# Seven block products in place of eight, and one step for the remainder, in the cosine layer of a Fourier and two-layer network kernel

## The chip, the core and the metric

The kernel runs on one core of one Trainium2 chip. Its engines work side by side: TensorE (PE in the rows; PEld is its weight load), VectorE (DVE), ScalarE (ACT), GpSimd (POOL) and SyncE (SP), which here only starts transfers. They share SBUF, and TensorE writes its sums to PSUM, in which the kernel takes tiles of one or two banks of 128 x 512 floats, and VectorE and ScalarE read them there. The metric is the device time of the whole launch in microseconds; less is better.

## The reference

`x` is 4 x 3008 tokens of 256 values, `w_in` is 256 x 2048 and `w_out` is 2048 x 256 in both layers, all of it in 32-bit floats:

```
X = Re FFT(FFT(x, axis=1), axis=2)             # attn, per batch
t = relu(X @ moe_w_in)                         # layer 1
x2 = (t * t) @ moe_w_out
h = x2 @ moe2_w_in                             # layer 2, first product
y = (h * cos(h)) @ moe2_w_out                  # layer 2, second product
```

## The kernel before, in words

Every product keeps float precision by splitting each factor into a high and a low part in the 32-bit matmul format: wh x xh, wh x xl and wl x xh, three matmuls on TensorE for one product. Tokens lie along the columns, features along the 128 partitions. The real part of the transform pairs a token with its mirror image, so the work goes by pairs: `BLOCKS` holds 12 blocks of 512, 512 and 480 pairs (the last 484), and the first product of layer 1 gives a sum and a difference from which `l1_add` makes both tokens of a pair.

Layer 1 runs over 12 blocks x 16 slices of 128 hidden features: `l1_mm1` (6 matmuls, line 550), `l1_add` (three VectorE operations, lines 557 and 235, the latter in the helper `tt`), `l1_act` (three ScalarE operations, lines 567 to 570), `l1_lo` (four GpSimd pieces, line 580) and `l1_mm2` (12 matmuls, line 592). At a block's end `l1_out` (lines 608 to 621) makes a high and a low part of the sums and stores both to the array `o_dram`, of which `load_o` reads both parts for layer 2.

Layer 2 runs over `HALVES`, 24 groups of up to 512 columns, x `NS` = 8 steps of two slices each. A step is `l2_mm1` (12 matmuls, lines 635 to 645) into a PSUM tile of two banks (one of the two `h` buffers, or every third time `acc1`), `l2_n` (ScalarE, line 650: h / 2 pi rounded to an integer n), `l2_r` (VectorE, line 658, twice: r = h - n C1 - n C2, with C1 + C2 = 2 pi), `l2_cos` (ScalarE, lines 665 and 666: the absolute value and the sine that gives the cosine), `l2_g` (VectorE, lines 671 and 235: times h), `l2_hi` (ScalarE, line 676) and `l2_lo` (GpSimd, line 683): the high and low part of the result g, and `l2_mm2` (12 matmuls, line 695) into `acc0`; after eight steps `l2_out` (lines 698 to 705) copies the sums out and stores them.

The weights of layer 2 are converted from their 64-bit form during layer 1 by `conv_w2`, stored, and loaded back by `load_w2` when layer 2 nears. No scheduler decides the order: every piece of work is registered by `at(t, fn, name)` with a time in units of steps, the table `TIMES` replaces some of these times by name, and `od.issue()` sorts all of them and writes the instructions. Each engine then runs its own in that order. A step's second product stands 4.3 steps behind its first one (`LAG + 1.3`, with 3 for `LAG`), and the other stages lie between.

Of the kernel before, what the change touches and what calls it, by code (L numbers as in the profile page):

```python
# [91 lines left out]

@with_exitstack
def kernel(ctx: ExitStack, tc: tile.TileContext, x, x128, cs, tab0, tab1, w_in1, w_out1, w_in2, w_out2, out):
    nc = tc.nc
# [539 lines left out]
    def l2_mm1(k, i):
        w = HALVES[k][1]
        hi, lo = xt[2, k]
        step = NS * k + i
        a = ps_a.tile([P, 2, BLK], F32, name="acc1") if step > LAG and step % 3 == 1 else ps_h.tile([P, 2, BLK], F32, name="h")
        for j in range(2):  # L640
            for m in range(2):
                wh, wl = (w_in_t([c[p] for c in wi2], m, 2 * i + j) for p in range(2))
                for q, (st, mv) in enumerate(((wh, hi), (wh, lo), (wl, hi))):
                    nc.tensor.matmul(a[:, j, :w], st, mv[:, m, :w], start=m == 0 and q == 0, stop=m == 1 and q == 2)  # L644
        hs[k, i] = a
# [365 lines left out]
```

## Time and profile before

| | us |
|---|---|
| three runs | 1927.09, 1930.08, 1930.56 |
| their median | 1930.08 |
| span of the profiled execution | 1925.3 |
| TensorE busy | 1886.7 (98%) |
| ScalarE busy | 1481.3 (77%) |
| VectorE busy | 1341.9 (70%) |
| GpSimd busy | 1074.6 (56%) |

The span runs from the first to the last instruction that the profiler recorded; the time of a run has in addition what lies around it. Layer 1 gives way to layer 2 between about 883 and 896 us of the span: before that stand the transform and layer 1, behind it some 1,025 us of layer 2. Durations in the rows are of single instructions or of short runs of them (x4 stands for four in a row).

### The profile page before, as it was taken

How to read it: one execution, taken by the hardware profiler on the slowest of the kernel's cores; microseconds unless marked ns; L12 is line 12 of the kernel's file. 1: busy time of each engine (PE TensorE's matmuls, PEld its weight loads, DVE VectorE, ACT ScalarE, POOL GpSimd, SP SyncE). 2: the span in 40 equal slices, each digit the busy share in tenths (PEclk: the TensorE clock that was granted, in tenths of full speed). 3: DMA queues.
4: the chain of work that ended last, by engine and by line, in shares of the span. 5: the costliest groups of instructions: out<-in, count | busy, mean ns of one | idle time of the engine just before them, and what ended most of it. 6: DMA issues, size and time to landing. Idle time of an engine off the chain costs nothing.

```text
span 1925.3 us, 23825 instructions
## 1 busy us (share of the span) xinstructions
PE 1886.7 (98%) x8544; PEld 1571.1 (82%) x8544; DVE 1341.9 (70%) x1566; ACT 1481.3 (77%) x1537; POOL 1074.6 (56%) x1004
## 2 busy tenths in 40 slices
PE   5899999999999999999999999999999999999999
PEld 3678888888888888888888888888888888888887
DVE  6889858768576776666666666666666666666666
ACT  3788778777788888887777777777777777777776
POOL 1667778777677777774444444444444444444442
PEclk9899999999999999999999999999999999999999
DMA  8564434334434434344011011100110001011100
GB/s 278 177 245 148 157 111 165 141 123 168 149 131 128 150 107 140 116 162 159 33 43 44 33 32 33 44 32 32 46 42 33 32 32 43 33 34 34 52 12 21
DMA packets 76345, 177.85 MB, mean 92 GB/s; under 512 B 9168, under 2 KB 32736, under 8 KB 76132
## 3 DMA queue, kind: packets, MB, share of 16 engines
q1 hardware_dynamic: 73812, 168.27, 25.9%
q0 software_dynamic: 1840, 6.73, 1.1%
q8 instruction: 67, 1.10, 0.2%
q10 hardware_dynamic: 576, 1.35, 0.2%
q14 instruction: 50, 0.41, 0.1%
HBM read 117.53 MB, written 63.42 MB: 94 GB/s over the span
## 4 chain that ended last, share of the span: by engine, by line
PE 81%; DVE 1%; issue 0%; ACT 0%; DVEq 0%; ACTq 0%
PE acc L695 27%; PE h L644 18%; PE acc L592 18%; PE acc L644 9%; PE h L550 9%; PE h L333 1%; DVE s L235 0%; DVE inT L235 0%; DVE u L557 0%; DVE ol L235 0%; ACT oh L618 0%; DVE o L703 0%; ACT o L702 0%; DVEq L235 0%; DVE dl L235 0%
## 5 line engine op out<-in xcount | busy, mean ns | idle before, releaser
L683 POOL TENSOR_TENSOR gl<-r,gh 128x1024 fp32r<-128x1024 f32 (+2 forms) x189 | 445.4, 2356 | 574.5 <-ACT gh L676 564.5
L580 POOL TENSOR_TENSOR gl<-s,gh 128x256 fp32r<-128x256 f32 (+2 forms) x768 | 591.2, 801 | 218.9 <-ACT gh L570 194.0
L658 DVE SCALAR_TENSOR_TENSOR r<-n,h 128x1024 f32<-128x1024 int32 (+2 forms) x129 | 154.7, 1199 | 219.1 <-ACT n L650 201.3
L567 ACT ACTIVATE s<-s 128x1024 f32<-128x1024 f32 (+2 forms) x192 | 199.5, 1039 | 89.3 <-DVE s L235 88.8
L235 DVE TENSOR_TENSOR s<-u,h 128x512 f32<-128x512 f32 (+2 forms) x384 | 242.8, 674 | 25.7 <-POOL gl L580 3.8
L650 ACT ACTIVATE n<-h 128x1024 int32<-128x1024 f32 (+2 forms) x129 | 130.3, 1010 | 160.5 <-PE h L644 160.4
L592 PE MATMUL acc<-gh,wbh 128*128 128x512 f32 (+2 forms) x768 | 237.2, 390 | 0.7 <-DVE ol L235 0.7
L592 PE MATMUL acc<-gl,wbh 128*128 128x512 f32 (+2 forms) x768 | 235.9, 388 | 1.4 <-POOL gl L580 1.3
L658 DVE SCALAR_TENSOR_TENSOR r<-n,r 128x1024 f32<-128x1024 int32 (+2 forms) x192 | 231.6, 1206 | 6.6
L592 PE MATMUL acc<-gh,wbl 128*128 128x512 f32 (+2 forms) x768 | 235.1, 387 | 0.0
L557 DVE SCALAR_TENSOR_TENSOR u<-zb,wc,h 128x512 f32<-128x512 f32 (+2 forms) x192 | 140.6, 732 | 130.2 <-PE h L550 129.2
L666 ACT ACTIVATE r<-r,halfpi 128x1024 f32<-128x1024 f32 (+2 forms) x192 | 218.3, 1137 | 6.2
L568 ACT ACTIVATE s<-s 128x1024 f32<-128x1024 f32 (+2 forms) x192 | 200.6, 1045 | 6.1
L570 ACT ACTIVATE gh<-s 128x1024 fp32r<-128x1024 f32 (+2 forms) x192 | 200.5, 1044 | 6.1
L695 PE MATMUL acc<-gh,wbh 128*128 128x512 f32 (+2 forms) x768 | 202.9, 386 | 0.0
L695 PE MATMUL acc<-gh,wbl 128*128 128x512 f32 (+2 forms) x768 | 202.9, 386 | 0.0
L695 PE MATMUL acc<-gl,wbh 128*128 128x512 f32 (+2 forms) x768 | 202.8, 386 | 0.0
L644 PE MATMUL h<-xh,wah 128*128 128x512 f32 (+2 forms) x516 | 199.2, 386 | 0.0
L644 PE MATMUL h<-xl,wah 128*128 128x512 f32 (+2 forms) x516 | 199.2, 386 | 0.0
L644 PE MATMUL h<-xh,wal 128*128 128x512 f32 (+2 forms) x516 | 199.1, 386 | 0.0
L665 ACT ACTIVATE r<-r 128x1024 f32<-128x1024 f32 (+2 forms) x192 | 198.2, 1032 | 0.0
L676 ACT ACTIVATE gh<-r 128x1024 fp32r<-128x1024 f32 (+2 forms) x192 | 197.1, 1027 | 1.1 <-DVE r L658 0.8
(125 smaller groups left out, 3257.6 us busy)
## 6 DMA issues: line engine op xcount, KB each, us to landing
inT<-x_in SPq DMA_DIRECT2D x18, 512.0 KB, 7.6
oh<-oh SPq DMA_DIRECT2D x16, 512.0 KB, 3.5
ol<-ol SPq DMA_DIRECT2D x16, 512.0 KB, 2.8
xh<-oh SPq DMA_DIRECT2D x16, 512.0 KB
xl<-ol SPq DMA_DIRECT2D x16, 512.0 KB, 4.7
y_out<-o SPq DMA_DIRECT2D x32, 256.0 KB, 2.1
mid<-w_in SPq DMA_DIRECT2D x14, 511.5 KB, 4.4
mid<-w_out SPq DMA_DIRECT2D x14, 511.0 KB, 4.1
```

The costliest lines, as they stand in the source:

```text
L235: nc.vector.tensor_tensor(out=out, in0=in0, in1=in1, op=op)
L567: nc.scalar.activation(s[:, :, :w], s[:, :, :w], AF.Relu)
L568: nc.scalar.activation(s[:, :, :w], s[:, :, :w], AF.Square)
L570: nc.scalar.activation(hi[:, :, :w], s[:, :, :w], AF.Copy)
L580: nc.gpsimd.tensor_tensor(out=lo[:, n, cols], in0=s[:, n, cols], in1=f32(hi)[:, n, cols], op=ALU.subtract)
L592: nc.tensor.matmul(accs[1, k][m][:, n, :w], wt, g[:, n, :w], start=begin and i == 0, stop=end and i == 2)
L644: nc.tensor.matmul(a[:, j, :w], st, mv[:, m, :w], start=m == 0 and q == 0, stop=m == 1 and q == 2)
L658: nc.vector.scalar_tensor_tensor(out=r[:, :, :w], in0=n[:, :, :w], scalar=-c, in1=src[:, :, :w], op0=ALU.mult, op1=ALU.add)
L665: nc.scalar.activation(r[:, :, :w], r[:, :, :w], AF.Abs)
L666: nc.scalar.activation(r[:, :, :w], r[:, :, :w], AF.Sin, bias=halfpi, scale=-1.0)
L683: e.tensor_tensor(out=lo[:, :, :w], in0=r[:, :, :w], in1=f32(hi)[:, :, :w], op=ALU.subtract)
L695: nc.tensor.matmul(accs[2, k][:, m, :w], w_out_t([c[part] for c in wo2], f, m), g[:, j, :w], start=f == 0 and q == 0, stop=f == NF - 1 and ...
```

## The change

**Seven products.** The weights' slices of a step (two, each 256 deep) and a span of columns form a 2 x 2 grid of blocks on either side: A is w_in of layer 2 (rows are the two slices, columns the two halves of the depth), B is x2 (rows are the halves of the depth, columns two groups of tokens). In place of the eight products A_ik B_kj the new code takes seven, M1 to M7, of sums of blocks. `SPANS` has 12 spans of 512 column pairs (the last 388) in place of the 24 groups, so that a span's two groups are the two column blocks. Sums on the weights' side (S1 to S4) are made once in layer 1, by `sums_w2`. Sums on the side of x (T1X to T4X) are made for every span by `diff`, on GpSimd (on VectorE for the first), and each of the seven right-hand factors is then split by `x_hi` (ScalarE, line 700) and `x_lo` (VectorE, line 704).

**Two banks with partial sums.** The products go to two single banks, b0 and b1. In b0 stand M1, then M1 + M6, then that + M7, then that + M4, which is the corner C21 of the result; in b1 M5, then M5 + M3, and then anew M2. Between them partial sums are copied to SBUF: x1 = M1 (ScalarE, line 730), x2 = M1 + M6 and x5 = M5 (VectorE, line 732). The corners of h are then C12 = b1 + x2, C11 = b1 + x1 and C22 = b0 + x5 (VectorE, `tt`, line 237) and C21 = b0 (ScalarE, line 742), all in SBUF.

**The remainder in one step.** `l1_out` now scales by 1 / 2 pi (a ScalarE pass, line 668, and a VectorE pass, line 669, for the two parts of the constant) and stores one float array. So h comes in turns, and n is h rounded, in a pair of PSUM banks `pp` (line 747), the remainder r = h - n is one operation (line 751), and the sine takes 2 pi as its scale (line 757), without an absolute value. `l2_g` of the first slice pair stays on VectorE and that of the second goes to GpSimd (line 762); high part line 768, low part line 773. n1, r1, c1, g1, h1, l1 and n2 to l2 name these stages for the two row blocks. `l2_mm2` comes in eight pieces m0 to m7 of three matmuls (line 785), so that they can stand between the products. `l2_out` multiplies by 2 pi.

**The order.** A step now has 16 x 128 x 128 blocks of work on two groups of columns, as two steps had before. Its length is `STEP` = 2.5 of the units of `at`, and a table `OFF` places each piece. `l1_mm1` takes its three matmuls in another order, its last two slices go to `pp`, and layer 1's last five second products stand among the first products of layer 2, which begin 1.5 units before layer 1's last slot. From `TIMES` eight entries of the steps 187 to 192 are gone.

The core of the diff:

```diff
-HALVES = [(2 * c + n * w, w) for c, w in BLOCKS for n in range(2)]
+SPANS = [(c, min(BLK, NPAIR - c)) for c in range(0, NPAIR, BLK)]
-    o_dram = [dram.tile([2, P, NCOL], F32, name=f"o{p}") for p in "hl"]
+    o_dram = dram.tile([2, P, 2, NPAIR], F32, name="o")
...
+    def sums_w2(c, j):
...
+            tt(o[0], b[1][0], b[1][1], ALU.add)
+            tt(o[1], o[0], b[0][0], ALU.subtract)
+            tt(o[2], b[0][0], b[1][0], ALU.subtract)
+            tt(o[3], b[0][1], o[1], ALU.subtract)
...
     def l1_out(k, m):
-        nc.scalar.activation(hi, src, AF.Copy)
-        tt(lo, src, f32(hi), ALU.subtract)
...
+        nc.scalar.activation(o, src, AF.Copy, scale=PER2)
+        nc.vector.scalar_tensor_tensor(out=o, in0=src, scalar=PER1, in1=o, op0=ALU.mult, op1=ALU.add)
+        nc.sync.dma_start(out=o_dram[m][:, :, c:c + w], in_=o)
...
+    def diff(k, j, e):
+        a, b = {T1X: ("b12", B11), T3X: (B22, "b12"), T2X: (B22, T1X), T4X: (B21, T2X)}[j]
+        e.tensor_tensor(out=cols_of(k, j), in0=cols_of(k, a), in1=cols_of(k, b), op=ALU.subtract)
+    def x_hi(k, j):
...
+        nc.scalar.activation(x[:, 0], cols_of(k, j), AF.Copy)
+    def x_lo(k, j):
+        x = right[k, j]
+        nc.vector.tensor_tensor(out=x[:, 1], in0=cols_of(k, j), in1=f32(x)[:, 0], op=ALU.subtract)
+    M1, M2, M3, M4, M5, M6, M7 = (A11, B11), (A12, B21), (S4, B22), (A22, T4X), (S1, T1X), (S2, T2X), (S3, T3X)
+    def product(k, i, b, pair_of, start):
...
+        for q, (st, mv) in enumerate(((wl, 0), (wh, 1), (wh, 0))):
+            nc.tensor.matmul(bank["b"][b][:, :w], st, x[:, mv], start=start and q == 0, stop=q == 2, skip_group_check=True)
+    def copy_of(k, i, x, b, e):
...
+        src = bank["b"][b][:, :w]
+        if e is nc.scalar:
+            nc.scalar.activation(u, src, AF.Copy)
+        else:
+            nc.vector.tensor_copy(u, src)
+    def corner(k, i, j, n, b, x):
+        src, dst = bank["b"][b][:, :SPANS[k][1]], h_of(k, i, j)[:, n]
+        if x is None:
+            nc.scalar.activation(dst, src, AF.Copy)
+        else:
+            tt(dst, src, us[k, i, x], ALU.add)
     def l2_n(k, i, j):
-        nc.scalar.activation(n[:, :, :w], hs[k, i][:, :, :w], AF.Copy, scale=1.0 / (2.0 * math.pi))
+        nc.scalar.activation(bank["p"].bitcast(I32)[:, :, :SPANS[k][1]], hs[k, i, j], AF.Copy, bias=0.25)
     def l2_r(k, i, j):
-        for c, src in ((C1, hs[k, i]), (C2, r)):
-            nc.vector.scalar_tensor_tensor(out=r[:, :, :w], in0=n[:, :, :w], scalar=-c, in1=src[:, :, :w],
-                                           op0=ALU.mult, op1=ALU.add)
+        nc.vector.scalar_tensor_tensor(out=r, in0=bank["p"].bitcast(I32)[:, :, :SPANS[k][1]], scalar=-1.0, in1=hs[k, i, j],
+                                       op0=ALU.mult, op1=ALU.add)
     def l2_cos(k, i, j):
-        nc.scalar.activation(r[:, :, :w], r[:, :, :w], AF.Abs)
-        nc.scalar.activation(r[:, :, :w], r[:, :, :w], AF.Sin, bias=halfpi, scale=-1.0)
+        dst = r if j else bank["p"][:, :, :SPANS[k][1]]
+        nc.scalar.activation(dst, r, AF.Sin, bias=halfpi, scale=TURN)
     def l2_g(k, i, j):
-        tt(r[:, :, :w], r[:, :, :w], h[:, :, :w], ALU.mult)
+        if j:
+            (V if ends(k, i) else G).tensor_tensor(out=r, in0=r, in1=h, op=ALU.mult)
+        else:
+            tt(r, bank["p"][:, :, :SPANS[k][1]], h, ALU.mult)
...
+    OFF = {"M5": -0.267, "x5": -0.173, "M1": 0.0, "M3": 0.133, "x1": 0.154, "M6": 0.267, "x2": 0.362, "C12": 0.447, "M7": 0.467,
+           "M2": 0.533, "C11": 0.635, "C22": 0.701, "n1": 0.757, "M4": 0.8, "r1": 0.893, "C21": 0.895, "n2": 1.052, "r2": 1.177,
+           "c1": 1.321, "c2": 1.431, "g1": 1.513, "g2": 1.567, "h1": 1.656, "l1": 1.818, "m0": 1.867, "h2": 1.951, "l2": 2.075,
+           "m1": 2.2, "m2": 2.334, "m3": 2.401, "m4": 2.601, "m5": 2.668, "m6": 2.934, "m7": 3.068}
...
+            hi = {B11: 2.82, B22: 3.82, T1X: 4.82, T2X: 6.82, T3X: 7.3, B21: 7.82, T4X: 8.3}
+            lo = {B11: 3.76, B22: 4.76, T1X: 5.76, T2X: 7.32, T3X: 7.76, B21: 8.32, T4X: 8.34}
+            dif = {T1X: 4.5, T3X: 5.5, T2X: 6.5, T4X: 7.5}
```

How the order stands, on TensorE in the middle of layer 2. Before, twelve matmuls of the first product (line 644) stand in one block, ahead of and behind twelve of the second (line 695); the rows are the end of one block of each:

```order
L644 MATMUL acc1_8897<-xh_8603,wah_7941 128x512
L644 MATMUL acc1_8897<-xl_8604,wah_7941 128x512
L644 MATMUL acc1_8897<-xh_8603,wal_7942 128x512
L695 MATMUL acc0_8650<-gh_8855,wbh_8326 128x512 [waits Activation_49]
L695 MATMUL acc0_8650<-gh_8855,wbh_8326 128x512 x3
L695 MATMUL acc0_8650<-gh_8855,wbl_8327 128x512 x4
L695 MATMUL acc0_8650<-gl_8857,wbh_8326 128x512 [waits Pool_49]
L695 MATMUL acc0_8650<-gl_8857,wbh_8326 128x512 x3
L644 MATMUL h_8944<-xh_8603,wah_8074 128x512 [waits DVE_49,PE_49]
```

After, at a boundary of two spans: the products M5, M4 and M1 (line 713, by the banks that they write) stand with units of three or six of the second product (line 785) around them:

```order
L713 MATMUL b1_8151<-x_8593,wal_7814 128x512 [waits DVE_49]
L713 MATMUL b1_8151<-x_8593,wah_7813 128x512 x2
L713 MATMUL b0_8150<-x_8867,wal_7814 128x512 [waits DVE_49,Activation_49]
L713 MATMUL b0_8150<-x_8867,wah_7813 128x512 x2
L785 MATMUL acc0_8359<-gh_8895,wbh_8385 128x512 [waits Activation_49]
L785 MATMUL acc0_8359<-gh_8895,wbh_8385 128x512
L785 MATMUL acc0_8359<-gh_8895,wbl_8386 128x512
L785 MATMUL acc1_8415<-gh_8843,wbh_8385 128x512 x2
L785 MATMUL acc1_8415<-gh_8843,wbl_8386 128x512
L713 MATMUL b0_8150<-x_8436,wal_7814 128x512 [waits Activation_49]
L713 MATMUL b0_8150<-x_8436,wah_7813 128x512 x2
```

What moved: the first product no longer stands in blocks of twelve into banks of its own; every third or sixth matmul belongs to another bank, and most groups of the first product wait for a reader of the bank that they write.

VectorE, at the same place. Before, a step holds two remainders and one product with h:

```order
L658 SCALAR_TENSOR_TENSOR r_10200<-n_10198,acc1_10172 128x1024 [waits Activation_49,Pool_49]
L658 SCALAR_TENSOR_TENSOR r_10200<-n_10198,r_10200 128x1024 [waits DVE_49]
L235 TENSOR_TENSOR r_10156<-r_10156,h_10125 128x1024 [waits Activation_49]
L658 SCALAR_TENSOR_TENSOR r_10237<-n_10235,h_10210 128x1024 [waits Activation_49,Pool_49]
L658 SCALAR_TENSOR_TENSOR r_10237<-n_10235,r_10237 128x1024 [waits DVE_49]
L235 TENSOR_TENSOR r_10200<-r_10200,acc1_10172 128x1024 [waits Activation_49]
```

After, from x2 to x5 and the two remainders, with the splits of x (line 704) of the next span between them:

```order
L732 COPY x_8792<-b0_8150 128x512 [waits PE_49]
L237 TENSOR_TENSOR h_8798<-b1_8151,x_8792 128x512 [waits DVE_49]
L237 TENSOR_TENSOR r_8755<-pp_8152,h_8717 128x1024 [waits Activation_49]
L237 TENSOR_TENSOR h_8798<-b1_8151,x_8775 128x512 [waits PE_49]
L237 TENSOR_TENSOR h_8818<-b0_8150,x5_8750 128x512
L704 TENSOR_TENSOR x_8785<-oin_8374,x_8785 128x512
L732 COPY x5_8832<-b1_8151 128x512 [waits DVE_49,PE_49]
L751 SCALAR_TENSOR_TENSOR r_8837<-pp_8152,h_8798 128x1024 [waits Activation_49,Pool_49]
L751 SCALAR_TENSOR_TENSOR r_8859<-pp_8152,h_8818 128x1024 [waits Activation_49,Pool_49]
L704 TENSOR_TENSOR x_8830<-oin_8375,x_8830 128x512
L704 TENSOR_TENSOR x_8867<-oin_8374,x_8867 128x512 [waits Activation_49]
```

What moved: the copies and corners stand on VectorE between the stages of the cosine, and a split stands ahead of x5, or behind the second remainder and so ahead of the next x2.

TensorE where the layers meet. Before, the first product of layer 1's last slices (line 550) alternates with blocks of its second product (line 592), and the first product of layer 2 follows in blocks of twelve; after, M5, M4 and M1 of layer 2 stand directly behind each other, between blocks of twelve of layer 1's second product (now line 644):

```order
L713 MATMUL b1_8151<-x_7946,wal_7814 128x512 [waits DVE_49]
L713 MATMUL b1_8151<-x_7946,wah_7813 128x512 x2
L713 MATMUL b0_8150<-x_8102,wal_7814 128x512 [waits DVE_49]
L713 MATMUL b0_8150<-x_8102,wah_7813 128x512 x2
L713 MATMUL b0_8150<-x_7870,wal_7814 128x512 [waits Activation_49]
L713 MATMUL b0_8150<-x_7870,wah_7813 128x512 x2
L644 MATMUL acc0_7765<-gh_8191,wbh_1315 128x484 x2
L644 MATMUL acc0_7765<-gh_8191,wbl_1316 128x484 x2
L644 MATMUL acc0_7765<-gl_8193,wbh_1315 128x484 [waits Pool_49] x2
```

What moved: M1 of a step follows M4 of the step before without another matmul between them.

## Rows read from the trace of the kernel before

**Rows 1.** The page's first part: busy us of each engine, share of the span, instructions.
```profile
PE 1886.7 (98%) x8544; PEld 1571.1 (82%) x8544; DVE 1341.9 (70%) x1566; ACT 1481.3 (77%) x1537; POOL 1074.6 (56%) x1004
```

**Rows 2.** Stretches, us: PE, PEld, DVE, ACT, POOL busy (instructions), PEclk, DMA share, GB/s.
```profile
750.00:800.00 50.00, 50.00 (x221) 41.31 (x220) 33.62 (x52) 43.22 (x45) 38.07 (x51) 1.00 0.39 131
1000.00:1050.00 50.00, 50.00 (x223) 41.43 (x222) 33.92 (x30) 38.19 (x39) 21.60 (x9) 1.00 0.09 31
```

**Rows 3.** Timeline of PE in layer 2 (start us, duration us), line 695.
```profile
942.51 1.07 PE L695 MATMUL acc<-gh,wbh 128*128 128x512 f32 x4
...
947.95 1.07 PE L695 MATMUL acc<-gh,wbh 128*128 128x512 f32 x4
...
1083.11 1.03 PE L695 MATMUL acc<-gh,wbh 128*128 128x480 f32 x4
...
1088.31 1.03 PE L695 MATMUL acc<-gh,wbh 128*128 128x480 f32 x4
```

**Rows 4.** Groups by line and shape, 910 to 1910: busy us, mean ns | idle before.
```profile
L683 POOL TENSOR_TENSOR gl<-r,gh 128x1024 fp32r<-128x1024 f32 x126 | 302.3, 2399 | 378.4 <-ACT gh L676 378.4
...
L666 ACT ACTIVATE r<-r,halfpi 128x1024 f32<-128x1024 f32 x124 | 143.1, 1154 | 4.0
L676 ACT ACTIVATE gh<-r 128x1024 fp32r<-128x1024 f32 x126 | 131.5, 1044 | 0.0
...
L235 DVE TENSOR_TENSOR r<-r,h 128x1024 f32<-128x1024 f32 x82 | 99.5, 1214 | 0.0
L658 DVE SCALAR_TENSOR_TENSOR r<-n,h 128x1024 f32<-128x1024 int32 x81 | 98.9, 1221 | 140.4 <-ACT n L650 135.3 <-POOL gl L683 5.1
L650 ACT ACTIVATE n<-h 128x1024 int32<-128x1024 f32 x81 | 83.3, 1029 | 102.6 <-PE h L644 102.5
...
L703 DVE COPY o<-acc 128x512 f32<-128x512 f32 x16 | 11.1, 692 | 1.1
...
L702 ACT ACTIVATE o<-acc 128x512 f32<-128x512 f32 x16 | 9.2, 577 | 0.0
```

**Rows 5.** Waits, 910 to 1910: engine and line, whom for: us, times, longest.
```profile
ACT n L650 <- PE h L644: 157.0, 124, 1.5
```

**Rows 6.** Timeline of one step of layer 2, with the wait in brackets.
```profile
1007.56 0.39 PE L644 MATMUL h<-xh,wal 128*128 128x512 f32 x1
...
1007.99 1.03 ACT L650 ACTIVATE n<-h 128x1024 int32<-128x1024 f32 x1 [1.33 <-PE h L644]
...
1009.12 1.22 DVE L658 SCALAR_TENSOR_TENSOR r<-n,h 128x1024 f32<-128x1024 int32 x1 [1.83 <-ACT n L650]
```

**Rows 7.** Timelines of two places in layer 1 where engines follow each other.
```profile
880.30 0.72 DVE L557 SCALAR_TENSOR_TENSOR u<-zb,wc,h 128x484 f32<-128x484 f32 x1 [1.02 <-PE h L550]
881.15 1.23 DVE L235 TENSOR_TENSOR s<-u,h 128x484 f32<-128x484 f32 x2
...
51.38 1.29 DVE L235 TENSOR_TENSOR s<-u,h 128x512 f32<-128x512 f32 x2 [2.25 <-POOL gl L580]
...
52.72 0.50 PE L550 MATMUL h<-xh,wah 128*128 128x512 f32 x1 [1.90 <-DVE s L235]
...
53.06 0.39 PE L550 MATMUL h<-xl,wah 128*128 128x512 f32 x1
```

**Rows 8.** Tile dl (count: shortest/median/longest ns, first, last start), then a timeline.
```profile
L235 DVE TENSOR_TENSOR dl<-inT,dh x18: 685/1053/1287, 180.8 to 469.2; 128x512 fp32r<-128x512 f32 x18
L235 DVE TENSOR_TENSOR dl<-in,dh x4: 687/690/692, 26.1 to 41.2; 128x512 fp32r<-128x512 f32 x4
...
886.36 2.72 POOL L580 TENSOR_TENSOR gl<-s,gh 128x242 fp32r<-128x242 f32 x4 [0.27 <-ACT gh L570]
...
888.48 1.68 DVE L658 SCALAR_TENSOR_TENSOR r<-n,r 128x1024 f32<-128x1024 int32 x1
```

**Rows 9.** Groups by line and shape, 0 to 900, of layer 1.
```profile
L580 POOL TENSOR_TENSOR gl<-s,gh 128x256 fp32r<-128x256 f32 x512 | 400.2, 814 | 151.2 <-ACT gh L570 136.8 <-DVE s L235 6.0 <-PE acc L333 5.3
...
L235 DVE TENSOR_TENSOR s<-u,h 128x512 f32<-128x512 f32 x256 | 164.6, 685 | 18.7 <-POOL gl L580 3.8 <-DVE u L557 0.9 <-POOL zl L405 0.2
```

More of the change, by code (lines that the diff above doesn't have):

```diff
@@ L520, in load_w2, with left @@
         (wi2 if name == "in" else wo2).append(parts)
+    win, wie = {}, []
+    A11, A12, A22, S1, S2, S3, S4 = range(7)
+    def left(j, i):
+        c, s = i // 2, i % 2
+        if j < S2:
+            return [p[:, j * 2 * P + s * P:j * 2 * P + (s + 1) * P] for p in wi2[c]]
+        return [p[:, j - S2, s * P:(s + 1) * P] for p in wie[c]]
     gs, accs = {}, {}
-    xt, uv, ss = {}, {}, {}
+    xt, uv, ss, bank = {}, {}, {}, {}
     parts, part_dram = {}, {}
@@ L635, in l2_mm1 @@
[L635 to L645, printed above, removed]
@@ L679, in l2_lo @@
-    def l2_lo(k, i, e=nc.gpsimd):
-        w = HALVES[k][1]
-        hi, r = gs[2, k, i], rs.pop((k, i))
-        lo = buf("gl2", "gl", F32R, late["pool"], 4)
-        e.tensor_tensor(out=lo[:, :, :w], in0=r[:, :, :w], in1=f32(hi)[:, :, :w], op=ALU.subtract)
-        gs[2, k, i] = hi, lo
-    def l2_mm2(k, i):
-        w = HALVES[k][1]
-        if i == 0:
-            accs[2, k] = ps_a.tile([P, 2, BLK], F32, name="acc0")
-        hi, lo = gs.pop((2, k, i))
-        for q, (part, g) in enumerate(((0, hi), (1, hi), (0, lo))):
-            for m in range(2):
-                for j in range(2):
-                    f = 2 * i + j
-                    nc.tensor.matmul(accs[2, k][:, m, :w], w_out_t([c[part] for c in wo2], f, m), g[:, j, :w],
-                                     start=f == 0 and q == 0, stop=f == NF - 1 and q == 2)
@@ new lines, in x_hi @@
+    def x_hi(k, j):
+        tag = XTAGS[(7 * k + j) % 10]
+        x = buf(tag, "x", F32R, late["pool"] if tag in ("cv", "xc") else work, XTAGS.count(tag))[:, :, :SPANS[k][1]]
+        right[k, j] = x
+        nc.scalar.activation(x[:, 0], cols_of(k, j), AF.Copy)
[3 more added lines that the diff above has]
+    M1, M2, M3, M4, M5, M6, M7 = (A11, B11), (A12, B21), (S4, B22), (A22, T4X), (S1, T1X), (S2, T2X), (S3, T3X)
@@ new lines, in l2_hi, with l2_lo, l2_mm2 @@
+    def l2_hi(k, i, j):
+        gs[2, k, i, j] = hi = gh_buf()[:, :, :SPANS[k][1]]
+        nc.scalar.activation(hi, rs[k, i, j], AF.Copy)
+    def l2_lo(k, i, j):
+        hi, r = gs[2, k, i, j], rs.pop((k, i, j))
+        lo = (buf("B1", "gl", F32R) if j and i % 2 else gl_buf())[:, :, :SPANS[k][1]]
+        (V if ends(k, i) else G).tensor_tensor(out=lo, in0=r, in1=f32(hi), op=ALU.subtract)
+        gs[2, k, i, j] = hi, lo
+    def l2_mm2(k, i, n):
+        m, j, half = n // 4, n // 2 % 2, n % 2
+        w = SPANS[k][1]
+        if i == 0 and j == half == 0:
+            accs[2, k, m] = ps_a.tile([P, 2, BLK], F32, name=f"acc{m}")
+        f = 2 * i + j
+        hi, lo = gs[2, k, i, j]
+        for q in range(3 * half, 3 * half + 3):
+            part, g = ((0, hi), (1, hi), (0, lo))[q // 2]
+            nc.tensor.matmul(accs[2, k, m][:, q % 2, :w], w_out_t([c[part] for c in wo2], f, m), g[:, q % 2],
+                             start=f == 0 and q < 2, stop=f == NF - 1 and q >= 4)
@@ L858, with open_banks @@
             else:
-                at(i + LAG - 0.55, lambda k=k, m=m: l1_out(k, m), ("out", k, m))
+                at(i + LAG - 0.55 if k < NB - 1 else L2S + 4.05 + 0.4 * m, lambda k=k, m=m: l1_out(k, m), ("out", k, m))
                 if f0:
                     at(i + LAG - 2, lambda k=k, m=m: load_part(k, m), ("load_part", k, m))
+    def open_banks():
+        h_ctx.close()
+        ps_b = ctx.enter_context(tc.tile_pool(name="ps_b", bufs=1, space=PSUM))
+        bank["b"] = [ps_b.tile([P, BLK], F32, name=f"b{n}") for n in range(2)]
+        bank["p"] = ps_b.tile([P, 2, BLK], F32, name="pp")
     def open_late():
@@ L871 @@
         conv_w2(OPEN + 1.5 + SPAN * i, SPAN, *job)
-    T2S = NF * NB
+    at(T2S - 2.25, open_banks)
     for c in range(NCH):
@@ L981, in _token_columns @@
         pair = b * JB + np.arange(JB)
-        k = np.searchsorted([c for c, _ in BLOCKS], pair, side="right") - 1
-        c, w = (np.array([BLOCKS[i][n] for i in k]) for n in range(2))
-        plus = c + pair
-        minus = plus + w
+        plus = pair
+        minus = NPAIR + pair
         own, mirrored = np.where(flip, plus, minus), np.where(flip, minus, plus)
```

211 lines of the change are left out of this document (143 added, 68 removed).

## The prediction

> **What bounds the kernel now.** I read the busy shares first [rows 1]: TensorE is busy for 98% of the span, so the reader looks there first and asks whether it also runs without gaps. The busy time by stretches says yes: in layer 1 and in layer 2 alike a stretch of 50 us holds 50.00 us of TensorE at a granted clock of 1.00, the upper level, while VectorE has 34 us, ScalarE 38 and GpSimd 22 in layer 2 [rows 2]. The waits of layer 2 agree: its six rows name ScalarE, VectorE and GpSimd as those who wait, one of them ScalarE for the product h [rows 5], and TensorE in none. So the time of layer 2 is the number of matmul slots times the length of a slot. One block of 24 matmuls takes 947.95 - 942.51 = 5.44 us at 512 columns, 0.2267 us a slot, and 5.20 us, 0.2167 a slot, at 480 [rows 3]; the two differ by 0.3125 ns a column, so I take 0.2179 for 484 columns and 0.188 for 388.
>
> **Matmul slots: -64.3 us.** Before, layer 2 has 24 column groups of 8 steps with 24 matmuls: 192 x (16 x 0.2267 + 6 x 0.2167 + 2 x 0.2179) = 1029.7 us. After, it has 12 spans of 8 steps, and the order shows 45 matmuls in a step, 21 for the first product (7 x 3) and 24 for the second: 360 x (11 x 0.2267 + 0.188) = 965.4 us. The difference is 64.3 us, and it is worth its full length only if nothing makes TensorE wait.
>
> **A full step of 10.20 us, and what has to fit.** The seven products go through two banks that are read half-way, so TensorE now depends on a read within its own step. I count in units of three matmuls, 0.68 us. From its order, M1 begins at 0, M3 at 1.36, M6 at 2.72, M7 at 4.76, M2 at 5.44, M5 of the next step at 7.48, M4 at 8.16, M1 again at 10.20; second-product units fill the rest. A reader starts 0.20 us after the last slot ends (1007.79 to 1007.99), VectorE 0.10 after ScalarE ends [rows 6], VectorE 0.13 after its own earlier result, and TensorE 0.05 after VectorE, with a first slot that is 0.11 longer [rows 7]. The operations are priced by the nearest rows: copy from PSUM 0.69 on VectorE and 0.58 on ScalarE [rows 4], a sum with a PSUM input 0.69 [rows 9].
> - M6 to M7 through the copy x2: 0.20 + 0.69 + 0.16 = 1.05 of 1.36 us, 0.31 to spare.
> - M6 to M2 through x2 and the sum C12: 0.20 + 0.69 + 0.13 + 0.69 + 0.16 = 1.87 of 2.04, 0.17 to spare, the tightest.
> - M2 to M5 through C11: 1.05 of 1.36, 0.31 to spare. M4 to M1 through the ScalarE copy C21: 0.94 of 1.36, 0.42 to spare. M1 to M6 through x1: 0.94 of 2.04.
>
> The one shared pair of banks pp passes through two roundings, two remainders, a sine and a product: 2 x 1.03 + 2 x 1.22 + 1.15 + 1.21 [rows 4] and six handoffs of about 0.1, 7.5 us of 10.2. ScalarE has 2 x (1.03 + 1.15 + 1.04) + 2 x 0.58 and about 0.7 for the splits of x and the output, 8.3 us; VectorE 5 x 0.69 + 2 x 1.22 + 1.21 and about 0.9, 8.0; GpSimd 3 x 2.40 and 0.6 for the differences of x, 7.8. Two operations have no row. Rounding into PSUM: the nearest row rounds out of it, 1.03; 1.0 to 1.5 lies within the spare time of that chain. A multiplication on GpSimd: nearest is its subtraction, 2.40; from a little less up to 3.4 it stays hidden, since the second product wants that result about a microsecond after it is there. One remainder step for two and no absolute value remove work only from engines that nobody waited for: 0 us by themselves, but without them VectorE would hold 10.4 us and ScalarE 10.4, more than a step.
>
> So a bare step fits, and its cost is 0.
>
> **The splits of x: +18 us (3 to 38).** Seven times in a span VectorE subtracts with both inputs in SBUF (L704), placed between the operations above. Such a subtraction of 512 columns took 0.69 us in the early stage and 1.05 in the median beside a busy GpSimd, at most 1.29; a remainder with both inputs in SBUF took 1.22, but 1.68 the one time GpSimd was busy when it started [rows 8]: it ended about 1.1 us after GpSimd's piece did. In layer 1 GpSimd works in pieces of 0.81 us [rows 9]; in layer 2 in single instructions of 2.40 [rows 4]. If the mean wait of 0.36 grows with the length of the piece, it is 0.36 x 2.40 / 0.81 = 1.07 here. Four of the seven stand between C22 and x5. Behind them wait x5, the remainder r1, the rounding n2 and the copy x1, which M6 needs at 12.92: from the end of C22 at 7.6 that is 7.6 + 0.6 + 0.69 + 1.22 + 0.1 + 1.03 + 0.58 + 0.16 = 12.0, less some 0.2 for neighbours that overlap on an engine, so about 1.15 us to spare. With a wait spread evenly up to 2.40 and GpSimd busy for three quarters of the time, the overshoot is on average 0.75 x 1.25 x 1.25 / 2 / 2.40 = 0.24 us each, 1.0 a span. The other three stand just before x2, two of them in a row: 0.6 us a span. That makes 1.6 us in each of 11 spans, 18 us. Without any wait it is about 0.3 a span, 3 us; with the longest wait at three of the four places, 3 x 1.2, less what is then off the other three, 3.5 a span, 38 us.
> The Trainium skill says in "SBUF — State Buffer", section "Who interferes with whom", that a VectorE instruction with two SBUF inputs and a GpSimd instruction that reads SBUF exclude each other for the whole of the one that began first. The row of 1.68 us agrees in kind; against an instruction of 2.40 us no row shows it, and by the rule the sum would take its upper end.
>
> **Layer 2's start: +6.4 us (3 to 10).** Before, it has no gap (the stretches beside [rows 2]). After, the first steps have no second product of layer 2 to fill in, and layer 1's last five second products stand among them as blocks of twelve. I laid the first three steps out by the order of PE, ACT and DVE. M6 of step 0 needs x1, which stands on ScalarE behind layer 1's three activations of about 1.0 us each (1.04 for 1,024 columns [rows 4], these have 968): 0.8 us late. M1 of step 1 follows M4 at once and needs C21: 0.20 + 0.58 + 0.16, 0.95. M5 of step 2 needs C11, which stands on VectorE behind layer 1's last output (L669, waiting for the ScalarE pass L668 and that for layer 1's last product): 0.20 + 1.0 + 0.1 + 1.2 + 0.7 + 0.16 against 1.36, 1.85 late. The second output, x5 and x1 then come 0.55, 0.7 and 1.5 late; from step 3 on the spare times above hold.
>
> **The rest: +2.7 us.** At the end, the last step's chain (C11, rounding, remainder, rounding, remainder, sine, product, high part, about 7.9 us at 388 columns) outlasts the eleven units of 0.56 us that TensorE still has, by 1.7 (1 to 4). In layer 1 the weights get sums, some 19 us of VectorE spread over 160; that engine has 33.6 of 50 us there and TensorE does not wait [rows 2]: 1 us (0 to 3). Fewer transfers (one array in place of a high and a low one) are hidden either way: 0.
>
> **Sum.** 1925.3 - 64.3 + 18 + 6.4 + 1.7 + 1 = 1888.1 us of span. The median of the runs, 1930.1, lies 4.8 above the profiled span, and I keep that: 1893 us.
>
> **Rivals.**
> 1. The splits miss GpSimd. Whether a split comes before or after GpSimd begins the low part l1 is decided by some 0.05 to 0.1 us in my layout, and it repeats in each span. If they always come first, 18 becomes 3: 1878 us. For it: they are short and stand early on their queue; against it: GpSimd is busy for 7.8 of 10.2 us.
> 2. Each one loses: VectorE then stands up to 2.3 us behind a running l1, 38 in place of 18: 1913 us. For it: the 1.68 us row; against it: a delay in one step shifts the next step's meeting. This is where the exclusion stated by the page named above would lead.
> 3. The two banks become the bound. If every handoff from TensorE through a reader and back costs d more than the 0.35 us that I read, three of them lie in one loop (through C12, C11 and C21) and lose 3d - 0.17 - 0.31 - 0.42 a step. At d = 0.43 that is 0.40 us, times 94 steps the whole gain; at d = 0.6 it is 85 us: 1978 us, slower. For it: no row of before shows TensorE waiting for a reader in every step, or a bank read between two halves of a sum. Against: the handoffs that the rows show differ from each other by about 0.1 us, not 0.4.
>
> That the change does not do what it says I leave out: the order holds the 45 matmuls.
>
> **How the numbers follow.** The forecast, 1884 to 1902, 0.45; rival 1, 1868 to 1884, 0.25; rival 2, 1902 to 1918, 0.16; rival 3, 0.08; the start, the end or layer 1 costing 15 us or more beyond their bounds, 0.06, mostly still faster. The range reaches over the first three down to 1870 and up to 1918; above it lie rival 3 and half of the last, below it little, since 1865.8 is the time with no wait at all. This kernel can be told from no change by about 0.2%, 4 us. Faster by more: 0.45 + 0.25 + 0.16 + 0.03 = 0.89; within: 0.02; slower: 0.09.
>
> **What would show it.** In the profile after, a full step should take 10.2 us, steps with a split between C22 and x5 up to 11.4, and the waits should name M6 behind x1 and M7 behind x2 (L713 for L730 and L732) with some 18 us in all; L704 should be longer than 0.69 us where GpSimd runs. If plain steps take 10.5 us or more with M2, M5 or M1 waiting, rival 3 is at work. Six to seven us of gaps should lie where the layers meet. It would all be wrong if the granted clock fell to its lower level, for which I see no gap long enough.

## The result and the profile after

The changed kernel takes 1905.4 us (median of four runs, 1904.97 to 1909.47) against 1929.9 for the kernel before beside it: 24.5 us less by the medians; the ratio of the runs is 0.9881, 95% interval 0.9867 to 0.9895. The forecast was 1893 in a range of 1870 to 1918: the direction is right and the time within the range, but 12 us above the forecast, in the stretch of rival 2 (1902 to 1918).

The page of after, its first part, as in [rows 1]; the span is 1902.9 us:

```profile
PE 1836.1 (96%) x8256; PEld 1507.2 (79%) x8256; DVE 1454.8 (76%) x1867; ACT 1443.0 (76%) x1618; POOL 1374.1 (72%) x1144
```

288 matmuls are gone, as counted, but TensorE is busy for 96% of the span in place of 98%. The stretch of layer 2 that answers to [rows 2] shows that it now waits there, at the same granted clock:

```profile
1000.00:1050.00 50.00, 48.77 (x215) 39.70 (x214) 38.39 (x42) 37.49 (x45) 40.52 (x19) 1.00 0.00 1
```

For whom, the waits of TensorE between 915 and 1810 us say (PE its matmuls, PEld its weight loads; us in total, times, longest). One wait can stand in both, so they are not added up:

```profile
PE b L713 <- ACT x L730: 18.8, 31, 0.6
PE b L713 <- DVE x L732: 2.8, 10, 0.3
...
PEld b L713 <- ACT x L730: 31.9, 31, 1.0
PEld b L713 <- DVE x L732: 7.0, 10, 0.7
PEld b L713 <- DVE h L237: 2.0, 10, 0.2
```

So M6 waits for the copy x1 31 times and M7 for the copy x2 ten times, the two that the prediction named. One such place, with the step ahead of it as the undisturbed one (M3 at 1290.79 and at 1300.98, M6 at 1302.35 and at 1313.33):

```profile
1290.79 0.39 PE L713 MATMUL b<-x,wel 128*128 128x512 f32 x1
...
1300.98 0.39 PE L713 MATMUL b<-x,wel 128*128 128x512 f32 x1
...
1302.35 0.39 PE L713 MATMUL b<-x,wel 128*128 128x512 f32 x1
...
1304.56 1.21 DVE L237 TENSOR_TENSOR r<-pp,h 128x1024 f32<-128x1024 f32 x1
1304.56 2.41 POOL L762 TENSOR_TENSOR r<-r,h 128x1024 f32<-128x1024 f32 x1 [0.35 <-ACT r L757]
...
1306.95 2.40 POOL L773 TENSOR_TENSOR gl<-r,gh 128x1024 fp32r<-128x1024 f32 x1
...
1307.15 2.75 DVE L704 TENSOR_TENSOR x<-oin,x 128x512 fp32r<-128x512 f32 x1
...
1309.82 0.68 DVE L732 COPY x<-b 128x512 f32<-128x512 f32 x1
...
1310.42 1.21 DVE L751 SCALAR_TENSOR_TENSOR r<-pp,h 128x1024 f32<-128x1024 int32 x1
...
1311.73 1.03 ACT L747 ACTIVATE pp<-h 128x1024 int32<-128x1024 f32 x1 [1.51 <-DVE r L751]
1312.69 0.58 ACT L730 ACTIVATE x<-b 128x512 f32<-128x512 f32 x1
...
1313.33 0.50 PE L713 MATMUL b<-x,wel 128*128 128x512 f32 x1 [0.62 <-ACT x L730]
```

The split (L704) starts at 1307.15, 0.20 us after GpSimd began l1 (L773, 1306.95 to 1309.35), and ends at 1309.90: 0.55 us after GpSimd does. It took 2.75 us in place of 0.68. Behind it stand x5, r1, n2 and x1, and M6 comes 10.98 us after the last one in place of 10.20, with a first slot that is 0.11 longer. In the two rows at 1304.56, VectorE's product and GpSimd's start together and take 1.21 and 2.41 us as always: one input of VectorE's lies in PSUM there.

The groups of after (905 to 1890 us, as in [rows 4]):

```profile
L773 POOL TENSOR_TENSOR gl<-r,gh 128x1024 fp32r<-128x1024 f32 x175 | 425.6, 2438 | 53.4 <-ACT gh L768 52.3
...
L762 POOL TENSOR_TENSOR r<-r,h 128x1024 f32<-128x1024 f32 x87 | 209.8, 2412 | 183.6 <-ACT r L757 162.9 <-PE acc L785 20.7
...
L747 ACT ACTIVATE pp<-h 128x1024 int32<-128x1024 f32 x173 | 176.0, 1017 | 49.5 <-DVE r L751 49.5
...
L732 DVE COPY x<-b 128x512 f32<-128x512 f32 x172 | 118.1, 687 | 71.0 <-PE b L713 70.9
L704 DVE TENSOR_TENSOR x<-oin,x 128x512 fp32r<-128x512 f32 x70 | 112.6, 1621 | 0.0
```

The two operations without a row of their own came out near the rows taken: rounding into PSUM 1.02 us, GpSimd's multiplication 2.41. Only the splits are off: 1.62 us on average, 0.93 more than a free one takes.

### The profile page after: what moved, and what is told of

Same layout as the page of the kernel before. It is cut to its first block, busy times and chain, and to the rows that moved or that the text cites. A ratio compares the mean times of both kernels' runs of the same rounds, so it can differ in the third digit from the quotient of the medians.

```text
span 1902.9 us, 23618 instructions
## 1 busy us (share of the span) xinstructions
PE 1836.1 (96%) x8256; PEld 1507.2 (79%) x8256; DVE 1454.8 (76%) x1867; ACT 1443.0 (76%) x1618; POOL 1374.1 (72%) x1144
## 4 chain that ended last, share of the span: by engine, by line
PE 63%; DVE 8%; issue 5%; ACT 3%; POOL 3%; DVEq 0%; ACTq 0%; POOLq 0%
PE b L713 18%; PE acc L785 18%; PE acc L644 18%; PE h L602 8%; DVE r L751 3%; DVE h L237 2%; POOL gl L773 2%; ACT pp L747 2%; DVE x L732 1%; PE h L335 1%; DVE x L704 1%; POOL r L762 1%; ACT x L730 1%; DVE s L237 0%; DVE u L609 0%
## 5 line engine op out<-in xcount | busy, mean ns | idle before, releaser
L773 POOL TENSOR_TENSOR gl<-r,gh 128x1024 fp32r<-128x1024 f32 (+1 forms) x190 | 454.1, 2396 | 58.8 <-ACT gh L768 57.7
L762 POOL TENSOR_TENSOR r<-r,h 128x1024 f32<-128x1024 f32 (+1 forms) x95 | 225.3, 2372 | 204.1 <-ACT r L757 183.5
L751 DVE SCALAR_TENSOR_TENSOR r<-pp,h 128x1024 f32<-128x1024 int32 (+1 forms) x192 | 229.5, 1195 | 112.4 <-ACT pp L747 108.7
L785 PE MATMUL acc<-gh,wbl 128*128 128x512 f32 (+1 forms) x768 | 264.7, 385 | 0.0
L644 PE MATMUL acc<-gh,wbh 128*128 128x512 f32 (+2 forms) x768 | 236.9, 390 | 0.7 <-DVE o L669 0.7
L644 PE MATMUL acc<-gl,wbh 128*128 128x512 f32 (+2 forms) x768 | 235.4, 387 | 1.5 <-POOL gl L632 1.3
L785 PE MATMUL acc<-gh,wbh 128*128 128x512 f32 (+1 forms) x768 | 233.8, 385 | 1.0 <-ACT gh L768 1.0
L644 PE MATMUL acc<-gh,wbl 128*128 128x512 f32 (+2 forms) x768 | 234.4, 386 | 0.0
L785 PE MATMUL acc<-gl,wbh 128*128 128x512 f32 (+1 forms) x768 | 233.5, 385 | 0.4 <-POOL gl L773 0.4
L713 PE MATMUL b<-x,wah 128*128 128x512 f32 (+1 forms) x768 | 233.6, 385 | 0.0
```

The source lines that it names most:

```text
L644: nc.tensor.matmul(accs[1, k][m][:, n, :w], wt, g[:, n, :w], start=begin and i == 0, stop=end and i == 2)
L713: nc.tensor.matmul(bank["b"][b][:, :w], st, x[:, mv], start=start and q == 0, stop=q == 2, skip_group_check=True)
L751: nc.vector.scalar_tensor_tensor(out=r, in0=bank["p"].bitcast(I32)[:, :, :SPANS[k][1]], scalar=-1.0, in1=hs[k, i, j], op0=ALU.mult, op1=AL ...
L762: (V if ends(k, i) else G).tensor_tensor(out=r, in0=r, in1=h, op=ALU.mult)
L773: (V if ends(k, i) else G).tensor_tensor(out=lo, in0=r, in1=f32(hi), op=ALU.subtract)
L785: nc.tensor.matmul(accs[2, k, m][:, q % 2, :w], w_out_t([c[part] for c in wo2], f, m), g[:, q % 2], start=f == 0 and q < 2, stop=f == NF - ...
```

## The experiments

Theory A is that of rival 2: a split that VectorE asks for while GpSimd runs an instruction that reads SBUF waits until that instruction ends, and the lateness runs through x5, r1, n2 and x1 to M6. All runs below stood beside the kernel before, which took 1928.5 us on the one chip used and 1928.8 on the other (medians).

**The same splits elsewhere.**

```diff
-            lo = {B11: 3.76, B22: 4.76, T1X: 5.76, T2X: 7.32, T3X: 7.76, B21: 8.32, T4X: 8.34}
+            lo = {B11: 4.0, B22: 5.0, T1X: 6.0, T2X: 7.0, T3X: 7.32, B21: 8.0, T4X: 8.34}
```

> The seven splits of x move to places at which the trace of after shows VectorE idle and GpSimd idle or about to end: between the first and the second remainder (five of them) and behind the second remainder, one at a time. Theory A, that a split waits for the whole GpSimd instruction that began 0.2 us ahead of it (2.75 us in place of 0.69 at three places a span) and the chain x5, r1, n2, x1 hands 0.89 us of it to M6, and that the two splits in a row ahead of x2 cost M7 0.55: the waits of M6 and M7 in steady spans, 34 us together, go, and full spans take 81.6 to 82.0 us in place of 85.0. Time 1905.4 - 34 + 1 = 1872 us (1868 to 1878). Theory B, that the cost is VectorE's own work, seven subtractions and not their meeting with GpSimd: the same work is still on VectorE, the waits move to other products and the time stays within 8 us of 1905.

Measured: 1870.4 us, ratio 0.9701 (0.9686 to 0.9715). Full spans take 81.63 us. The splits' group and the stretch, of this kernel:

```profile
L704 DVE TENSOR_TENSOR x<-oin,x 128x512 fp32r<-128x512 f32 x70 | 51.5, 736 | 0.0
```
```profile
1000.00:1050.00 50.00, 50.00 (x223) 41.38 (x222) 36.57 (x44) 37.87 (x45) 41.67 (x20) 1.00 0.00 1
```

As many splits, 0.74 us each, and TensorE has no gap in this stretch. So it was not VectorE's work that cost 35 us but where it stood.

**GpSimd's work in halves.**

```diff
-        (V if ends(k, i) else G).tensor_tensor(out=lo, in0=r, in1=f32(hi), op=ALU.subtract)
+        for n in range(2):
+            (V if ends(k, i) else G).tensor_tensor(out=lo[:, n], in0=r[:, n], in1=f32(hi)[:, n], op=ALU.subtract)
```

(and the product g2, line 762, likewise.)

> The splits stay where they are; each low part and product on GpSimd (1,024 columns, 2.40 us) is issued as two instructions of 512 columns. Theory A: a split waits for what is left of one instruction, about 1.0 us at most, in place of 2.0, and M6 has 1.17 us of spare time for it: the 28 us of M6's waits go, the 6.6 us of M7 (two splits in a row, neither of which waits) stay. Time 1905.4 - 28 = 1877 us (1873 to 1884, the upper end if two halves take 0.2 us longer than one whole). Theory C, that VectorE is slowed down in proportion while GpSimd works, whatever the size of its instructions: the splits stay near 2.7 us and the time within 6 us of 1905.

Measured: 1875.7 us, 0.9728 (0.9711 to 0.9744). The groups of this kernel:

```profile
L775 POOL TENSOR_TENSOR gl<-r,gh 128x512 fp32r<-128x512 f32 x352 | 466.9, 1351 | 22.8 <-ACT gh L769 22.4
...
L704 DVE TENSOR_TENSOR x<-oin,x 128x512 fp32r<-128x512 f32 x70 | 86.6, 1249 | 0.0
```

The splits stay where they were and now take 0.56 us longer than a free one, in place of 0.93; M6 waits no more, M7 still does. A slowdown in proportion (theory C) would have left them at 1.62. A half takes 1.35 us on average, 1.30 where no split holds it up, and two of these take 2.55 from the start of the first to the end of the second: cutting costs some 0.15 us an instruction, which nobody waits for here.

**GpSimd writes and doesn't read.**

```diff
-        (V if ends(k, i) else G).tensor_tensor(out=lo, in0=r, in1=f32(hi), op=ALU.subtract)
+        if j == 0 and not ends(k, i):
+            G.memset(f32(lo), 0.0)
+        else:
+            (V if ends(k, i) else G).tensor_tensor(out=lo, in0=r, in1=f32(hi), op=ALU.subtract)
```

> The first low part of a step (l1, GpSimd) is replaced by writing zeros to the same tile from the same engine, so this part of the second product is left out; splits and order stay. Theory A in the form that two instructions exclude each other only where both read SBUF: the splits at the three places take 0.7 us, M6 does not wait, M7 still loses 0.55 us a span: 1877 us (1872 to 1884). Theory D, that any GpSimd instruction that touches SBUF holds VectorE's two-input subtractions: the splits wait for the zeros as they did for the subtraction; if writing zeros takes as long, about 1905, if it takes 1 us, 1880.

Measured: 1869.5 us, ratio 0.9697 (0.9678 to 0.9716). The zeros (L774) take 0.96 us; a split that starts while they are written (timeline of this kernel) is not held:

```profile
1343.48 0.95 POOL L774 MEMSET gl<- 128x1024 f32 x1
...
1343.80 0.68 DVE L704 TENSOR_TENSOR x<-oin,x 128x512 fp32r<-128x512 f32 x1
```

If it had waited, it would have ended at 1344.98 (0.55 us behind the zeros, as in after); it ended at 1344.48. What I had wrong is M7: I put its 6.6 us down to two splits in a row, and nearly all of them went too. In this run the split ahead of them is not late, so the two in a row fit; M7's wait in after needs both. The run in halves agrees: there the split ahead of them still takes 1.77 us, and M7 still waits.

**One place earlier.**

```diff
-            lo = {B11: 3.76, B22: 4.76, T1X: 5.76, T2X: 7.32, T3X: 7.76, B21: 8.32, T4X: 8.34}
+            lo = {B11: 3.69, B22: 4.69, T1X: 5.69, T2X: 7.32, T3X: 7.69, B21: 8.32, T4X: 8.34}
```

> The four single splits move by one place only, ahead of the corner C22 in place of behind it; the two in a row ahead of x2 stay. Theory A: whoever asks first goes first. In after, a split was asked for 0.2 us after GpSimd began l1 and waited for all of it. One place earlier it is asked for while GpSimd is in g2, waits for the rest of that, some 0.4 us, and then l1 waits for the split; VectorE loses 0.4 us of 1.17 to spare and M6 does not wait. The 28 us go, the 6.6 of M7 stay: 1877 us (1873 to 1884). Rival E: in the steady cycle the split meets g2 or l1 wherever it stands between C11 and x5, and C22 behind it makes M4 late as well: within 8 us of 1905, or more.

Measured: 1894.4 us, 0.9822 (0.9806 to 0.9838), between the two. Its timeline:

```profile
1342.55 2.41 POOL L762 TENSOR_TENSOR r<-r,h 128x1024 f32<-128x1024 f32 x1 [1.78 <-ACT r L757]
...
1344.55 0.97 DVE L704 TENSOR_TENSOR x<-oin,x 128x512 fp32r<-128x512 f32 x1
1344.94 2.84 POOL L773 TENSOR_TENSOR gl<-r,gh 128x1024 fp32r<-128x1024 f32 x1
...
1345.44 0.68 DVE L237 TENSOR_TENSOR h<-b,x 128x512 f32<-128x512 f32 x1
...
1346.17 0.50 PE L713 MATMUL b<-x,wal 128*128 128x512 f32 x1 [0.23 <-DVE h L237]
```

The order of asking decides, as theory A has it: the split asked while GpSimd was in g2 (to 1344.96), took 0.97 us, and now l1 is the one that is held (2.84 in place of 2.40). M6 waits no more, and M7, whose 6.6 us I had expected to stay, hardly does either, as in the run with the zeros. But C22 stands behind the split, and M4 overwrites the bank that C22 reads: 44 times 0.49 us, 21.6 in all. That is the mechanism of rival E in the expectation, though the time lies below its range; I had priced VectorE's delay by M6's spare time alone, and M4's is smaller.

**What the two banks have to spare.** On the places of the first experiment:

```diff
-            nc.vector.tensor_copy(u, src)
+            for _ in range(2 if x == 2 else 1):
+                nc.vector.tensor_copy(u, src)
```

> On e1_places, VectorE makes the copy x2 twice, 0.69 us more between M6 and M7 in every step: what the two banks have to spare. By the prediction M6 to M7 has 0.31 us to spare and M6 to M2 0.17, so a step loses 0.69 - 0.17 = 0.5 us, 0.6 with the slower first slots behind a wait, in 95 steps 50 to 57: 1870 + 54 = 1924 us (1910 to 1936). If the spare times are 0.7 us or more, as they would be if readers start earlier than read, the time stays at 1870; if they are zero, 1870 + 95 x 0.8 = 1946.

Measured: 1920.1 us. The full steps take 10.69 to 10.74 us in place of 10.20 (10.91 in one step of a span): the second copy adds 0.73 us, and 0.5 us a step is lost, a first slot that is 0.11 longer among it. M7 starts 0.31 us later in the step, so 0.42 were spare to it, against 0.31 in the prediction; M2 starts 0.43 later, so 0.30 were spare through C12, against 0.17. The spare times of the step are right to about 0.1 us, and they are nearly as small as said.

**The remainder in two operations again.**

```diff
+        nc.vector.scalar_tensor_tensor(out=r, in0=bank["p"].bitcast(I32)[:, :, :SPANS[k][1]], scalar=0.0, in1=r,
+                                       op0=ALU.mult, op1=ALU.add)
```

> The remainder is made in two VectorE operations again (the second one adds zero times n), as in the kernel before; the absolute value stays away. The prediction said that one operation saves no time by itself but that VectorE would hold 10.4 us, more than a step, without it. Then x5, r1, n2, x1 to M6 is 1.3 us longer with 1.17 to spare and x2 stands behind two more operations: plain steps of 10.6 us or more in place of 10.2, and more where a split falls: 1905 + 90 x 0.45 = 1946 us (1930 to 1985), slower than the kernel before. If the remainder does not matter, plain steps stay at 10.2 and the time within 5 us of 1905.

Measured: 2019.5 us, 4.7% slower than the kernel before; the direction is as expected, the size is not (1930 to 1985). VectorE in one step of it, from one copy x5 to the next:

```profile
1276.05 0.69 DVE L732 COPY x<-b 128x512 f32<-128x512 f32 x1 [0.77 <-PE b L713]
1276.66 1.21 DVE L751 SCALAR_TENSOR_TENSOR r<-pp,h 128x1024 f32<-128x1024 int32 x1
1277.90 1.23 DVE L753 SCALAR_TENSOR_TENSOR r<-pp,r 128x1024 f32<-128x1024 int32 x1
1280.35 1.23 DVE L751 SCALAR_TENSOR_TENSOR r<-pp,h 128x1024 f32<-128x1024 int32 x1 [1.23 <-ACT pp L747]
1281.61 1.23 DVE L753 SCALAR_TENSOR_TENSOR r<-pp,r 128x1024 f32<-128x1024 int32 x1
1282.75 0.68 DVE L732 COPY x<-b 128x512 f32<-128x512 f32 x1
...
1287.27 0.69 DVE L732 COPY x<-b 128x512 f32<-128x512 f32 x1 [0.76 <-PE b L713]
```

A step is 11.22 us without any split (12 with one). I had counted what VectorE works, 10.4 us, and the chain to M6. But between the two remainders VectorE also stands still for n2 (1.23 us), since there is one pair pp, and x2, M7, M2 and M5 follow from there back to the next x5: a loop over VectorE, ScalarE and TensorE. With two operations it lacks 1.0 us; with one, by an estimate from these rows, it has 1.4 to spare (10.20 less 11.22 - 2.46 = 8.76). So the small edit carries the large one: seven products in this order without it lose 90 us against the kernel before.

**The remainder alone, in the kernel before.**

```diff
-        for c, src in ((C1, hs[k, i]), (C2, r)):
+        for c, src in ((2.0 * math.pi, hs[k, i]),):
```

> The kernel before with the remainder in one VectorE operation (h - n x 2 pi) and all else as it was. The prediction gives this part no time of its own, since TensorE does not wait for VectorE there: 1928.5 us, within 2. If VectorE's load mattered in the kernel before, the 192 x 1.2 us that it is relieved of would show as several us.

Measured: 1927.9 us, 0.9996 (0.9987 to 1.0006). VectorE has 22.58 us of 50 in the stretch from 1000 to 1050, in place of 33.92 [rows 2], and the time doesn't move: 0 by itself, as the prediction had it. That the absolute value is gone was not tried apart.

**Filling the start.** With the places of the first experiment, layer 1's last second products are cut into halves:

```diff
+            late_at = {11: (-0.19, 0.45), 12: (0.76, 1.6), 13: (2.2, 4.0), 14: (2.9, 4.59), 15: (3.4, 4.6)}
+            if k == NB - 1 and f > 10:
+                for m in range(2):
+                    at(L2S + late_at[f][m], lambda k=k, f=f, e=f == f1 - 1, m=m: l1_mm2(k, f, False, e, (m,)))
...
-                at(i + LAG - 0.55 if k < NB - 1 else L2S + 4.05 + 0.4 * m, lambda k=k, m=m: l1_out(k, m), ("out", k, m))
+                at(i + LAG - 0.55 if k < NB - 1 else L2S + (4.05, 5.0)[m], lambda k=k, m=m: l1_out(k, m), ("out", k, m))
```

> The places of e1_places, and where the layers meet the last five second products of layer 1 are cut into halves of six matmuls, which stand singly between products of layer 2 that depend on each other (M3 to M6, M6 to M7, M2 to M5, M4 to M1), with layer 1's last output 0.55 to 0.95 units later. Theory: the start's gaps are the handoffs of the two banks with nothing to fill them, and the last output ahead of x2: M6 of step 0, M1 of step 1, M5, M1, M3 and M6 around step 2, 5.2 us in e1_places as in after. With fillers 4 to 5 of them go: 1870.4 - 4.5 = 1866 us (1864.5 to 1869). Rival: the fillers wait themselves, for GpSimd's low parts of layer 1's last slices or for the buffers that they free late, and the time stays within 1.5 us of 1870.4 or rises.

Measured: 1865.7 us, 0.9672 (0.9658 to 0.9686), the fastest version: 63 us below the kernel before, 40 below the changed one. The stretch from 874 to 914 us where the layers meet, of after and of this kernel:

```profile
874.00:914.00 40.00, 36.46 (x157) 28.70 (x156) 24.11 (x32) 26.71 (x29) 19.60 (x21) 1.00 0.28 99
```
```profile
874.00:914.00 40.00, 39.14 (x173) 31.77 (x172) 25.61 (x34) 29.94 (x32) 23.12 (x24) 1.00 0.26 87
```

TensorE is busy for 39.1 us of the 40 in place of 36.5. The first experiment, on whose places this kernel builds, has 36.48 in the same stretch, so the gain is that of the start alone.

## Why the prediction was right, and where it was off

The sum again, each term as measured in after from the starts of its matmuls against 10.20 us a step:

| term | forecast | measured |
|---|---|---|
| slots | -64.3 | -68.4 (8,256 matmuls; 0.2267 us a slot at 512 columns, 0.1767 at 388) |
| bare step | 0 | 0 (steps without a split: 10.20) |
| splits of x | +18 (3 to 38) | +34.6: M6 28.1, M7 6.5 |
| start of layer 2 | +6.4 (3 to 10) | +5.2 |
| end | +1.7 (1 to 4) | +2.2 |
| layer 1 | +1 (0 to 3) | about +4, as the remainder of the sum, with small waits elsewhere |
| span | 1888.1 | 1902.9 |

**The step that failed is the size of the splits' term.** Place, chain and spare time were right: M6 lost 0.89 us where a split was 2.06 us longer, so 1.17 were spare, against "about 1.15". The wait was wrong. I spread it evenly over GpSimd's instruction, since a delay in one step shifts the next step's meeting. It does, but only between two states. A split that is asked for 0.2 us behind the start of l1 waits for all of it. The split of the step behind that is asked for 0.48 us ahead of l1, while g2 still runs; it goes first, and l1 is held. The next one meets l1 as the first did. The first two of these meetings, from the same span:

```profile
1349.37 2.41 POOL L773 TENSOR_TENSOR gl<-r,gh 128x1024 fp32r<-128x1024 f32 x1
1349.58 2.75 DVE L704 TENSOR_TENSOR x<-oin,x 128x512 fp32r<-128x512 f32 x1
...
1360.70 1.09 DVE L704 TENSOR_TENSOR x<-oin,x 128x512 fp32r<-128x512 f32 x1
1361.18 2.88 POOL L773 TENSOR_TENSOR gl<-r,gh 128x1024 fp32r<-128x1024 f32 x1
```

So three of the four places lose the most and one loses nothing, and in eight of the eleven full spans the loss is the same 3.43 us to two hundredths. In the fifth span the first split comes just ahead of l1 (1265.42 and 1265.56); there the second and the fourth lose and the third doesn't, and the span loses 2.5 us. This is the upper end of the term ("the longest wait at three of the four places", 38 us), on which rival 2 stands. The argument given against rival 2 was right about the shift, which spares one place in four, and wrong about the mean: nothing spreads the meetings evenly. That VectorE waits until GpSimd's instruction ends, the row of 1.68 us [rows 8] had said, and I took it for a single case. The Trainium skill, "SBUF — State Buffer", section "Who interferes with whom", says that the ports which the two engines share are an exclusive lock, that a VectorE instruction with two SBUF inputs contends for it with a GpSimd instruction that reads SBUF and not with one that only writes it, and that the order of issue decides who blocks. The traces agree in all three points: 2.75 us behind an instruction of 2.40, 2.88 or 2.84 the other way round, 0.68 beside the zeros.

**The slots** came out 4 us better than forecast. I had carried the difference between 512 and 480 columns on to 388 and taken 0.188 us a slot. A bare step of the last span, 45 matmuls, takes 7.95 us, 0.1767 a slot:

```profile
1855.77 0.34 PE L713 MATMUL b<-x,wal 128*128 128x388 f32 x1
...
1863.72 0.33 PE L713 MATMUL b<-x,wal 128*128 128x388 f32 x1
```

This, and a time that lies 2.5 us above the profiled span in place of 4.8, hid part of what the splits cost beyond the forecast. The 1865.8 us that the prediction calls the time with no wait at all was too high by the same 4 us; the fastest version takes 1865.7 and still waits at the start and the end. That the time came within the range is due to the range, which reached over rival 2, and a little to this luck.

**The start** is as laid out. The timeline of after has M6 of step 0, M1 of step 1 and M5 of step 2 behind the very readers named:

```profile
884.16 0.51 PE L713 MATMUL b<-x,wel 128*128 128x512 f32 x1 [0.50 <-ACT x L730]
...
893.85 0.50 PE L713 MATMUL b<-x,wal 128*128 128x512 f32 x1 [0.69 <-ACT h L742]
...
903.63 0.50 PE L713 MATMUL b<-x,wal 128*128 128x512 f32 x1 [0.78 <-DVE h L237]
...
910.15 0.50 PE L713 MATMUL b<-x,wel 128*128 128x512 f32 x1 [1.11 <-ACT x L730]
```

From start to start they lose 0.79, 0.97 and 1.06 us (0.8, 0.95 and 1.85 in the prediction). The third is smaller because L669 had ended when M2 was done. The second output then delays C21, x5 and x1 (the last row) and costs 0.37, 0.62 and 1.39 us, against 0.55, 0.7 and 1.5. The last run, which fills these places, took 4.7 us off the first experiment's time.

**Rival 3** did not come: plain steps are 10.20 and the run with the doubled copy shows the spare time that was read, within 0.1 us. It also shows how near it was: 0.7 us more in one reader costs 50.

**Layer 1** can't be told at this size. A matmul of one of its last first products starts at 861.24 us in after and at 859.89 in before, 1.35 later; but in the runs of this study M1 of step 0 starts between 880.5 and 884.6 us, in kernels that are nearly alike up to there. The 2.5 us between the median and the profiled span of after, in place of 4.8 before, are of that size too.

## What to carry to other kernels

When work is added to an engine with time to spare, price its place and not its length: look for what the other engine runs at that moment, whether both read SBUF with two inputs on VectorE's side, and who asks first. In a cyclic order such a meeting can come back at the same phase, as it did here in eight of eleven spans; then its cost is that of a few fixed meetings times the number of cycles, and a mean over all phases misses it. And where a change makes engines wait for each other within a step, sum the whole loop over all of them, with the time in which each stands still, before saying that an operation costs nothing.

## What the runs showed of the hardware that I had not expected

Where both read SBUF, and VectorE with two inputs, VectorE and GpSimd took turns in the order of asking: a split that asked 0.4 us before GpSimd's g2 ended ran ahead of l1, which was next on GpSimd, and l1 took 2.84 us. GpSimd needs 2.41 us for a subtraction or a product of 1,024 columns, 1.30 for 512 columns in the run in halves where no split held it up, and 0.96 for writing zeros to 1,024. And TensorE added to a bank that VectorE or ScalarE had just copied from, in the midst of a sum, at no more than the handoff: in the first experiment M7, with 0.31 us to spare by the prediction, stands 4.76 us behind M1 in 84 of the 85 full steps from step 3 on.
